# Attention plus token-mixing block: one query shift row folded and summed in one pass, and the output weights split into two parts for twelve matmuls

## The chip, the cores and the metric

The kernel runs on one core of a Trainium2 chip. The metric is the device time of one execution in microseconds (us). Before the change it is 433.37 us, the median of three runs (433.19 to 434.04).

## The reference

The input x has 2048 tokens (rows) of 448 channels. It passes through linear attention and then a mixer that mixes along the tokens; each is preceded by a layer norm whose scale and shift come from a small condition vector c, and each is added back through a gate:

```python
mod = silu(c) @ w_mod             # six rows of 448: sa, ca, ga, sb, cb, gb
h = layernorm(x) * (1 + ca) + sa
x = x + ga * A(h)
h = layernorm(x) * (1 + cb) + sb
x = x + gb * B(h)

def A(h):                         # 16 heads of 28 channels
    q, k, v = split(h @ wqkv)
    pq, pk = phi(q), phi(k)       # phi(t) = (t + 1 if t > 0 else exp(t)) + 1e-6
    kv, z = einsum(pk, v), sum(pk)            # per head, over all tokens
    return (pq @ kv / (pq @ z + 1e-6)) @ wo

def B(h):                         # along the tokens
    return w2.T @ gelu(w1.T @ h + b1) + b2
```

## The kernel before, in words

All arithmetic is in 32 bits. A matmul at full precision ("fp32") takes two passes on the matmul engine (PE). In most places the kernel instead splits each operand into a high part, rounded to the format `fp32r` by a copy on ACT, and a low part, the rest, and adds three products: high by high, high by low, low by high. `split(full, hi, lo)` (L82) makes the parts: a copy on ACT, a subtraction on DVE. A second way leaves DVE out: ACT copies the high part, ACT copies its negative into the low part, and a DMA from POOL's queue adds the full value to it. For the pieces of w1, `split_to` (L319) takes the second way for the pieces in `PIECE_DMA`; `split_end` (L315) issues their DMAs.

Every engine takes its instructions in the order in which the code emits them; there is no planner. Program order is therefore the schedule, and a step that waits holds up all that stands behind it on its engine.

The work has four stages.

1. *Projections and sums over tokens* (L560 to L825). The tokens come in 16 tiles of 128. In the loop `for t in range(4, NT)` (L682) PE projects tile t + 1 to keys (`project(t + 1, 1, "kp")`: ten matmuls, the third of which, "hl", needs the low part of the tile, made on DVE by `a_split_low`, L413), closes tile t (`close`, L437: one matmul with the norm's mean row `Wrow`), and adds an older tile to the four sums of keys by tokens (`a_outer`, L545: eleven matmuls). ACT and DVE turn the projections into phi(k), split them, and normalise and split x. From t = 10 on a query tile is projected per iteration as well (`a_q`).

   The layer norm's shift enters the projections by a row of `Wrow`. For q (j = 0) `row_part` (L275) accumulates on DVE a 128 x 448 tile `accb` of partial sums. In t = 9 `row_sum(0)` (L283: seven fp32r matmuls) and `row_bias(0)` (L289: one fp32 matmul of `sel_b` by `accb`) add everything up in a bank `rowb`, and `row_out(0)` (L292: a copy on ACT, a subtraction on DVE) writes it to `Wrow`.

2. *Joining* (L783 to L985). From the sums come `csum`, then the 112 x 448 products `kvb` (L814), which DVE multiplies by a mask into `kvm`. Wo lies in four parts `wo_sb[g]` of 112 rows, each multiplied on DVE by the gate `mods[2]` (L779, L791). Four fp32 matmuls `wp` (L968) multiply the groups of `kvm` by them. ACT copies each result to `wpg` (L970), eight DMAs from SP's queue regroup the rows into `wpr` (L977), and `wp_split` (L980) splits these into `wph` and `wpl`, which the next stage needs. Between these stand queries (`a_q`), and the pieces of w1, split two at a time (`split_to(2)`, 4, 6, 8).

3. *The loop over tiles* (L987, `for i in range(NT + LAG)`). For tile i, `b_transpose` (L857, writes `tq`) transposes the scaled queries `pn`, `b_high` (ACT) and `b_low`, `b_low_last` (DVE) split the result, and `b_out` (L887, `op`) multiplies it by `wph` and `wpl`. The `pn` of the next tile come from a chain on DVE with one step on POOL: `b_prod`, `b_sum`, `b_eps` (POOL), `b_recip`, `b_scale`. In DVE's order `b_low(i)` stands between `b_sum(i + 1)` and `b_recip(i + 1)`, so it is ahead of `pn` of tile i + 1. Norms, further queries and, from i = 5 on, the first product with w1 (`step`, `up`) are woven in. The iteration ends with `split_to(8 + max(0, i - 5))`.

4. *The mixer* (L1293 to L1333): the products `up` with w1, gelu, and the products `y` with w2.

Tiles of SBUF come from two pools, `slots` (74 buffers) and the smaller `tok` (27 buffers; helper `tslot`); a bank of PSUM comes from a pool of eight.

Of the kernel before, what the change touches and what calls it, by code (L numbers as in the profile page):

```python
# [20 lines left out]
DH = 28  # L21
EPS = 1e-5

PIECE_DMA = range(8, 18)
PRE_LOAD = {14: 2, 15: 4}
KV_LAG = 4
HIGH_AT = {13: (11, 12), 14: (13,), 15: (14, 15)}
# [24 lines left out]
def block_kernel(ctx: ExitStack, tc: tile.TileContext, x, xt, wqkv, wo, w1, b1, w2, c, wmod, wfirst, out):  # L52
# [50 lines left out]
    cst.tile([P, 112], F32, name="space")  # L103
# [12 lines left out]
    sel_s = cst.tile([P, ROWS], F32R, name="sel_s")  # L116
    rowst = []
    for i in range(RING):
        rowst.append(cst.tile([P, P], F32R, name=f"rowst{i}"))
# [115 lines left out]
    def mod_add(j):  # L235
        acc = macc[j]
        nc.vector.tensor_add(acc[:G - 64], acc[:G - 64], acc[64:])

    def mod_high(j):
        acc, both = macc[j], moving(slot, f"mh{j}")  # L240
        macc[j] = (both,)
        nc.scalar.activation(both[:64], acc[:64], AF.Copy)
        return lambda: nc.vector.tensor_sub(both[64:], acc[:64], both[:64].bitcast(F32))
# [43 lines left out]
            nc.tensor.matmul(rowb[j][:ROWS, :D], sel_s, w, start=(i == 0), stop=False)  # L287

    def row_bias(j):  # L289
        nc.tensor.matmul(rowb[j][:ROWS, :D], sel_b, accb.pop(j), start=False, stop=True)  # L290

    def row_out(j):  # L292
        ps, w = rowb.pop(j), Wrow[j]
# [157 lines left out]
    def a_exp(t, ps):  # L451
        a_exp1(t, ps)
        a_relu(t, ps)
# [223 lines left out]
    low()  # L677
    sum_end()
    a_split(7)
    wo_sb = []  # L680
    late = [t for t in range(NT) if t not in Q_EARLY.values()]
    for t in range(4, NT):  # L682
        if 5 < t < NT - 1:
            project(t + 1, 1, "kp")
        kp = close(t, 1) if t > 4 else kps[4]
        if t == 9:
            row_sum(0)
            row_bias(0)
        if t > 4:
            a_outer(t - KV_LAG)  # L690
        if t % 2 and 4 < t < NT - 2:
            a_transpose(t + 1)
        if t in Q_EARLY:
            a_q(Q_EARLY[t])
        if t == 12:
            mp = mod_sum2(2)
        pair = t % 2 and 7 < t + 3 < NT
        if pair:
            first, second, end = a_stats_dve((t + 3, t + 4))
            first(0)  # L700
        if 5 <= t < 9:
            w_low(0, t - 5)
        if pair:
            second(0)
        if 5 <= t < 9:
            row_part(0, t - 5)
        a_phi_q(t in Q_EARLY)
        if t == 9:
            a_exp(t, kp)
        if t % 2 and 4 < t < NT - 2:  # L710
            a_copy(t + 1)
            a_copy(t + 2)
        if t != 9:
            a_exp(t, kp)
        if 7 < t + 3 < NT:
            a_split_high(t + 3)
        a_pk_parts(t - 1)
        highs = HIGH_AT.get(t, (t - 2,))
        for i in highs[:1]:
            a_norm(i)  # L720
            a_high(i)
        if t % 2 == 0 and 4 < t < NT - 3:
            low = a_rows(t + 2)
        if t == 11:
            low2 = mod_high(2)
        for j, i in MOD_AT.get(t, ()):
            mod_add(j) if i is None else mod_part(j, i)
        if t == 14:
            low4()
        a_pk(t, kp)  # L730
        if t % 2 == 0 and 4 < t < NT - 3:
            low()
        if 7 < t + 3 < NT:
# [12 lines left out]
        if 4 <= t < 8:  # L746
            w_high(0, t - 4)
            if t == 7:
                w_row(0)
        if t == 9:  # L750
            row_out(0)
# [8 lines left out]
        if t == 10:  # L760
            mod_add(2)
        if t == 11:
            low2()
        if t == 13:
            low4 = mod_high(4)
        if t in (7, 10):
            load_mod(4 if t == 7 else 3)
        if t == 10:
            load_qkv(2, tslot)
        if t == 8:  # L770
            for g in range(4):
                w = tslot(f"wo{g}", parts=G)
                nc.sync.dma_start(w, wo[g * G:(g + 1) * G, :])
                wo_sb.append(w)
            b12 = cst.tile([P, NF + NT], F32, name="b12")
            nc.sync.dma_start(b12, b1)
            b1c, b2c = b12[:, :NF], b12[:, NF:]
        if t >= 13:
            nc.vector.tensor_mul(wo_sb[t - 13], wo_sb[t - 13], mods[2][:G])  # L779
        load_to(PRE_LOAD.get(t, 0))  # L780


    a_pk_parts(NT - 1)  # L783
    nc.vector.tensor_add(pksum[1], pksum[1], pksum[0])
    zs = (moving(slot, "zh"), moving(slot, "zl"))
    split(pksum[1], *zs)
    load_to(10)
    a_phi_q()
    a_outer(NT - 4)
    a_outer(NT - 3)  # L790
    nc.vector.tensor_mul(wo_sb[3], wo_sb[3], mods[2][:G])  # L791
# [12 lines left out]
    a_q(late.pop(0))  # L804
    csum = []
    for ch in range(4):
        csum.append(slot(f"cs{ch}"))
        nc.scalar.activation(csum[ch], cacc[ch][:, :D], AF.Identity, scale=col[1][:, ch:ch + 1])
        nc.vector.scalar_tensor_tensor(csum[ch], zb, col[0][:, ch:ch + 1], csum[ch], op0=ALU.mult, op1=ALU.add)
    a_phi_q()  # L810
    a_q(late.pop(0))
    split_to(6)
    mp = mod_sum2(4)
    kvb = bank("kvb")  # L814
    for ch in range(4):
# [6 lines left out]
    nc.vector.tensor_mul(kvm, kvb[:G, :D], mask)  # L822
# [7 lines left out]
    pns, phs, ys, opb, sums, nms, nm2s, rss, vss = {}, {}, {}, {}, {}, {}, {}, {}, {}  # L830

    dens, prods, lasts = {}, {}, {}

    def b_prod(t):
# [7 lines left out]
    def b_eps(t):  # L842
        nc.gpsimd.tensor_scalar_add(dens[t], dens[t], 1e-6)  # L843
# [4 lines left out]
    def b_scale(t):  # L848
        pn = pns.pop(t, None) or tslot(f"pn{t}", w=512)
        nc.vector.scalar_tensor_tensor(pn[:, :D].rearrange("p (h d) -> p h d", d=DH),  # L850
                                       pq[t].rearrange("p (h d) -> p h d", d=DH), 1e-6,
                                       dens.pop(t).unsqueeze(2).to_broadcast([P, H, DH]),
                                       op0=ALU.add, op1=ALU.mult)
        pns[t] = pn
        pq[t] = None

    def b_transpose(t):  # L857
        pn = pns.pop(t)
# [101 lines left out]
            del parts[k]  # L960

    a_q(late.pop(0))
    for fn in (b_prod, b_sum, b_eps, b_recip, b_scale):
        fn(0)
    mod_add(3)
    for g in range(4):
        wp = bank(f"wp{g}")
        nc.tensor.matmul(wp[:G, :D], kvm[:, g * G:(g + 1) * G], wo_sb[g], start=True, stop=True)  # L968
        wpg = tslot(f"wpg{g}", parts=G)
        nc.scalar.activation(wpg, wp[:G, :D], AF.Copy)  # L970
        if g == 0:
            Wpr += [tslot(f"wpr{ch}") for ch in range(4)]
        for ch in range(4):
            r0, r1 = max(ch * P, g * G), min(ch * P + P, (g + 1) * G)
            for p0 in (0, 64) if ch == 3 else (0,):
                if r0 < r1:
                    nc.sync.dma_start(Wpr[ch][p0 + r0 - ch * P:p0 + r1 - ch * P], wpg[r0 - g * G:r1 - g * G])  # L977
# [10 lines left out]
    for i in range(NT + LAG):  # L988
# [398 lines left out]
```

## Time and profile before

| | |
|---|---|
| median of three runs | 433.37 us |
| the profiled execution, its own time | 434.09 us |
| its span, from the first to the last instruction | 432.4 us |
| PE busy between 0 and 20 us | 18.89 us |
| PE busy between 20 and 40 us | 19.68 us |
| PE busy between 40 and 310 us | 270.0 of 270.0 us |
| PE busy between 310 and 432 us | 119.34 us |
| DVE busy between 40 and 60 us | 18.82 us |
| ACT busy between 120 and 130 us | 7.25 us |

A row of a timeline holds start and length in us, engine, line of code, instruction, result and operands, shapes, count, and in brackets the idle time of the engine before it with what ended that time. PEld is the load of a matmul's stationary operand. The start of a matmul in a stream is followed by the next 0.20 us later although its row says 0.36 us, since they are pipelined: the pitch from start to start is what one costs. The same holds, less strongly, for ACT and DVE.

### The profile page before, as it was taken

The page shows a single profiled execution, that of the slowest core. Times are in us where ns is not written, and L with a number is a line of the kernel's source. Part 1 is how long each engine was busy: PE and PEld are TensorE (multiplying, and loading weights), DVE is VectorE, ACT ScalarE, POOL GpSimd, SP SyncE. Part 2 cuts the span into 40 slices and gives each one's busy share as a digit, 9 for nine tenths or more (in the row PEclk, how much of TensorE's full clock was granted, in tenths as well). Part 3 has the DMA queues.
Part 4 walks back from the last instruction along what each step waited for, and adds up shares of the span by engine and source line. Part 5 has one row for each costly group of instructions (what it writes and reads, how often), then busy time and mean ns, then how long its engine had stood idle before and what let it go on. Part 6 is the DMA issues. An engine that isn't in the chain of part 4 may idle for free.

```text
span 432.4 us, 7216 instructions
## 1 busy us (share of the span) xinstructions
PE 427.9 (99%) x2331; PEld 398.0 (92%) x2331; DVE 365.1 (84%) x814; ACT 278.9 (65%) x595; POOL 120.1 (28%) x199
## 2 busy tenths in 40 slices
PE   8999999999999999999999999999999999999997
PEld 8888899999899999999999999999999999999996
DVE  4899987889899999998579695739799998898894
ACT  5799869658578899996755263537464664655550
POOL 4345444300026577775200000010113131132010
PEclk9999999999999999999999999999999999999999
DMA  8997997565300036354427461577379977986431
GB/s 282 385 337 162 239 264 162 89 206 193 86 1 0 26 74 148 74 125 97 145 85 244 142 212 50 166 203 210 79 193 214 207 159 159 214 170 144 85 46 41
DMA packets 63797, 66.14 MB, mean 153 GB/s; under 512 B 4816, under 2 KB 55312, under 8 KB 63760
## 3 DMA queue, kind: packets, MB, share of 16 engines
q1 hardware_dynamic: 54688, 50.90, 37.8%
q0 software_dynamic: 8784, 14.32, 20.8%
q10 hardware_dynamic: 288, 0.46, 0.4%
q8 instruction: 18, 0.29, 0.3%
q14 instruction: 19, 0.16, 0.1%
HBM read 46.30 MB, written 7.34 MB: 124 GB/s over the span
## 4 chain that ended last, share of the span: by engine, by line
PE 97%; DVE 1%; ACT 1%; issue 0%
PE y L1183 19%; PE up L951 10%; PE up L950 10%; PE up L952 10%; PE y L1184 9%; PE cacc L554 7%; PE qp L432 7%; PE op L893 7%; PE kp L432 6%; PE op L900 1%; PE warm L188 1%; PE tq L863 1%; PE qp L439 1%; PE kvb L818 1%; PE wp L968 1%; PE rowb L287 1%
## 5 line engine op out<-in xcount | busy, mean ns | idle before, releaser
L950 PE MATMUL up<-h2h,ph 128*128 128x448 f32 x224 | 81.2, 362 | 0.0
L951 PE MATMUL up<-h2l,ph 128*128 128x448 f32 x224 | 81.2, 362 | 0.0
L952 PE MATMUL up<-h2h,pl 128*128 128x448 f32 x224 | 80.8, 361 | 0.0
L1138 POOL DMA_DIRECT2D a<-a x16 | 14.2, 964 | 142.6 <-DMA pr<-in_B_w_dram 76.7
L950 PEld LDWEIGHTS up<-h2h,ph 128*128 128x128 f32 x224 | 42.0, 188 | 3.1
L952 PEld LDWEIGHTS up<-h2h,pl 128*128 128x128 f32 x224 | 41.9, 187 | 3.0
L951 PEld LDWEIGHTS up<-h2l,ph 128*128 128x128 f32 x224 | 42.0, 188 | 2.3
L84 DVE TENSOR_TENSOR pl<-pr,ph 128x512 fp32r<-128x512 f32 x46 | 30.7, 688 | 2.6 <-ACT ph L83 1.7
L1189 ACT ACTIVATE cc<-y 128x448 f32<-128x448 f32 x24 | 13.0, 546 | 26.7 <-PE y L1184 26.7
L1102 DVE TENSOR_TENSOR u<-u,mod 128x448 f32<-128x448 f32 x14 | 8.7, 623 | 23.0 <-ACT u L1101 22.8
L83 ACT ACTIVATE ph<-pr 128x512 fp32r<-128x512 f32 x46 | 27.6, 623 | 0.8 <-PE up L952 0.5
L1101 ACT ACTIVATE u<-up,b 128x448 f32<-128x448 f32 x14 | 8.8, 625 | 25.4 <-PE up L952 24.9
L432 PE MATMUL kp<-wh,hh 128*128 128x448 f32 x64 | 23.8, 377 | 0.0
L554 PE MATMUL cacc<-pkh,xh 128*128 128x448 f32 x64 | 23.6, 369 | 0.0
L432 PE MATMUL qp<-wh,hh 128*128 128x448 f32 x64 | 23.5, 368 | 0.0
L1203 POOL DMA_DIRECT2D out_dram<-yt x14 | 12.7, 909 | 37.3 <-DVE yt L1194 27.9
L843 POOL TENSOR_SCALAR den<-den 128x16 f32<-128x16 f32 x16 | 8.8, 548 | 44.2 <-DVE den L840 44.2
L554 PE MATMUL cacc<-pkl,xh 128*128 128x448 f32 x56 | 20.3, 362 | 0.0
L893 PE MATMUL op<-wph,pth 128*128 128x448 f32 x48 | 18.7, 390 | 0.0
L1144 DVE TENSOR_TENSOR a<-a,s 128x512 f32<-128x512 f32 (+1 forms) x32 | 18.5, 622 | 0.0
L83 ACT ACTIVATE s2h<-s 128x512 fp32r<-128x512 f32 (+1 forms) x16 | 8.3, 569 | 15.5 <-DVE s L1144 15.5
L1183 PE MATMUL y<-ub,a11h 128*128 128x448 f32 x56 | 18.2, 375 | 0.0
(235 smaller groups left out, 1383.7 us busy)
## 6 DMA issues: line engine op xcount, KB each, us to landing
pr<-in_B_w_dram SPq DMA_DIRECT2D x56, 256.0 KB, 3.1
a<-in_B_w_dram SPq DMA_DIRECT2D x32, 256.0 KB, 4.8
a<-in_B_w_dram SPq DMA_DIRECT2D x32, 192.0 KB, 4.7
xt<-in_xt_dram SPq DMA_DIRECT2D x16, 256.0 KB, 5.0
x<-in_A_x_dram SPq DMA_DIRECT2D x16, 224.0 KB, 5.0
wm<-in_B_wmod_dram SPq DMA_DIRECT2D x16, 196.0 KB, 5.2
out_dram<-x SPq DMA_DIRECT2D x14, 224.0 KB, 2.3
out_dram<-yt POOLq DMA_DIRECT2D x14, 224.0 KB, 6.1
```

The costliest lines, as they stand in the source:

```text
L83: nc.scalar.activation(hi, full, AF.Copy)
L84: nc.vector.tensor_sub(lo, full, hi.bitcast(F32))
L432: nc.tensor.matmul(pps[t, j][:, :D], a[:, ch * P:(ch + 1) * P], w, start=first, stop=False)
L554: nc.tensor.matmul(cacc[ch][:, :D], a[:, s], b, start=(t == 0 and i == 0), stop=(t == NT - 1 and i == len(todo) - 1))
L893: nc.tensor.matmul(opb[t][:, :D], a, b, start=(ch == n == 0), stop=False)
L950: nc.tensor.matmul(ps[:, :D], hi[:, sl], mh, start=first, stop=False)
L951: nc.tensor.matmul(ps[:, :D], hi[:, sl], ml, start=False, stop=False)
L952: nc.tensor.matmul(ps[:, :D], lo[:, sl], mh, start=False, stop=last)
L1138: nc.gpsimd.dma_start(w, a, accum_op=ALU.add)
L1144: nc.vector.tensor_tensor(w, raw2[q, a][i], raw2[q, b][i], op=op)
L1183: nc.tensor.matmul(ps[:, :D], h[:, s], w, start=opens and r == 0, stop=False, skip_group_check=True)
L1184: nc.tensor.matmul(ps[:, :HD], l[:, s], wh, start=False, stop=closes and r == PAIRS - 1, skip_group_check=True)
```

## The change

- *The query's shift row.* At the end of t = 8 `row_fold(0)` adds, on DVE, the lower 64 rows of `accb` to the upper 64. In t = 9 `row_high(0)` copies the 64 rows as a high part (ACT), copies `sel_b` to an fp32r tile `sel_r` (ACT), and subtracts the low part into the other 64 rows (DVE). `row_bias(0)` is then one fp32r matmul. `row_sum(0)` and `row_bias(0)` move from t = 9 to t = 10, behind `project(11)` and ahead of `close(10)`; `row_out(0)` follows that. In t = 9 `a_exp` moves ahead.
- *The sum of the gate row.* `mod_add(2)` moves from the end of t = 10 into t = 11.
- *Wo.* The products with `mods[2]` on DVE go. `wo_split` makes a high and a low part of each `wo_sb[g]`: two copies on ACT, one adding DMA from POOL's queue, in t = 14, t = 15 and, for two, behind the loop. The parts lie in the smaller pool.
- *kvm* is split too (ACT, DVE), and twelve fp32r matmuls replace four fp32 ones. The factor `mods[2]` comes in afterwards: DVE multiplies each result into `wpg` where ACT copied it.
- *Order.* The chain of `pn` of tile 0 moves from behind the `wp` stage to ahead of it. Of the pieces of w1, 4 is split just ahead of the `wp` matmuls, 5 between two `wp_split`, and 6 and 7 at the end of iteration i = 0, by the second way (`PIECE_DMA` now begins at 6).

```diff
-PIECE_DMA = range(8, 18)
+PIECE_DMA = range(6, 18)
...
     def row_bias(j):
-        nc.tensor.matmul(rowb[j][:ROWS, :D], sel_b, accb.pop(j), start=False, stop=True)
+        nc.tensor.matmul(rowb[j][:ROWS, :D], sel_r if j == 0 else sel_b, accb.pop(j), start=False, stop=True)
+
+    def row_fold(j):
+        acc = accb[j]
+        nc.vector.tensor_add(acc[:64], acc[:64], acc[64:])
+
+    def row_high(j):
+        acc, both = accb[j], moving(tslot, f"rb{j}")
+        nc.scalar.activation(both[:64], acc[:64], AF.Copy)
+        nc.scalar.activation(sel_r, sel_b, AF.Copy)
+        accb[j] = both
+        return lambda: nc.vector.tensor_sub(both[64:], acc[:64], both[:64].bitcast(F32))
...
+    def wo_split(g):
+        full, hi, lo = wo_sb[g], moving(tslot, f"woh{g}", parts=G), moving(tslot, f"wol{g}", parts=G)
+        nc.scalar.activation(hi, full, AF.Copy)
+        nc.scalar.activation(lo, hi.bitcast(F32), AF.Copy, scale=-1.0)
+        nc.gpsimd.dma_start(lo, full, accum_op=ALU.add)
+        wo_sb[g] = None
+        wos.append((hi, lo))
...
         if 5 < t < NT - 1:
             project(t + 1, 1, "kp")
-        kp = close(t, 1) if t > 4 else kps[4]
-        if t == 9:
+        if t == 10:
             row_sum(0)
             row_bias(0)
+        kp = close(t, 1) if t > 4 else kps[4]
+        if t == 10:
+            row_out(0)
...
+        if t == 9:
+            a_exp(t, kp)
+            row_high(0)()
...
+        if t > 13:
+            wo_split(t - 14)
...
         if t == 11:
+            mod_add(2)
             low2 = mod_high(2)
...
             low()
+        if t == 8:
+            row_fold(0)
         if 7 < t + 3 < NT:
             a_split_low(t + 3)
...
-        if t >= 13:
-            nc.vector.tensor_mul(wo_sb[t - 13], wo_sb[t - 13], mods[2][:G])
...
     a_pk_parts(NT - 1)
+    for g in (2, 3):
+        wo_split(g)
...
-    split_to(6)
+    b_prod(0)
+    b_sum(0)
+    b_eps(0)
     mp = mod_sum2(4)
...
     a_phi_q()
+    b_recip(0)
+    mod_out(4, mp)
     kvm = slot("kvm", parts=G)
     nc.vector.tensor_mul(kvm, kvb[:G, :D], mask)
-    mod_out(4, mp)
+    b_scale(0)
+    kvh, kvl = slot("kvh", dt=F32R, parts=G), slot("kvl", dt=F32R, parts=G)
+    split(kvm, kvh, kvl)
     load_to(PRE + MID + 3)
-    split_to(8)
...
     a_q(late.pop(0))
-    for fn in (b_prod, b_sum, b_eps, b_recip, b_scale):
-        fn(0)
     mod_add(3)
+    split_to(5)
+    wps = [bank(f"wp{g}") for g in range(4)]
+    for gs in ((0, 1), (2,), (3,)):
+        for i, (a, b) in enumerate(((kvh, 0), (kvh, 1), (kvl, 0))):
+            for g in gs:
+                nc.tensor.matmul(wps[g][:G, :D], a[:, g * G:(g + 1) * G], wos[g][b], start=(i == 0), stop=(i == 2))
     for g in range(4):
-        wp = bank(f"wp{g}")
-        nc.tensor.matmul(wp[:G, :D], kvm[:, g * G:(g + 1) * G], wo_sb[g], start=True, stop=True)
         wpg = tslot(f"wpg{g}", parts=G)
-        nc.scalar.activation(wpg, wp[:G, :D], AF.Copy)
+        nc.vector.tensor_mul(wpg, wps[g][:G, :D], mods[2][:G])
...
             for ch in range(4):
                 wp_split(ch)
+                if ch == 1:
+                    split_to(6)
```

More of the change, by code (lines that the diff above doesn't have):

```diff
@@ L101, in make_mask @@
                                 pattern=[[0, 4], [DH, 4], [0, DH]], channel_multiplier=-1)
-    cst.tile([P, 112], F32, name="space")
+    cst.tile([P, 14], F32, name="space")
     mhalf = cst.tile([P, 2], F32, name="mhalf")
@@ L116, in block_kernel @@
     sel_s = cst.tile([P, ROWS], F32R, name="sel_s")
+    sel_r = cst.tile([P, ROWS], F32R, name="sel_r")
     rowst = []
@@ L679, in block_kernel @@
     a_split(7)
-    wo_sb = []
+    wo_sb, wos = [], []
+    def wo_split(g):
[5 more added lines that the diff above has]
+        wos.append((hi, lo))
     late = [t for t in range(NT) if t not in Q_EARLY.values()]
@@ L707, in block_kernel @@
         a_phi_q(t in Q_EARLY)
-        if t == 9:
-            a_exp(t, kp)
         if t % 2 and 4 < t < NT - 2:
@@ L749, in block_kernel @@
                 w_row(0)
-        if t == 9:
-            row_out(0)
         if t == 12:
@@ L759, in block_kernel @@
             mod_part(2, t - 7)
-        if t == 10:
-            mod_add(2)
         if t == 11:
@@ L777, in block_kernel, with b_prod, b_sum, b_eps @@
             b1c, b2c = b12[:, :NF], b12[:, NF:]
-        if t >= 13:
-            nc.vector.tensor_mul(wo_sb[t - 13], wo_sb[t - 13], mods[2][:G])
         load_to(PRE_LOAD.get(t, 0))
+    pns = {}
+    dens, prods, lasts = {}, {}, {}
+    def b_prod(t):
+        prods[t] = tslot(f"pd{t}")
+        nc.vector.scalar_tensor_tensor(prods[t], pq[t], 1e-6, zb, op0=ALU.add, op1=ALU.mult)
+    def b_sum(t):
+        dens[t] = small.tile([P, H], F32, name=f"den{t}", tag="den")
+        nc.vector.tensor_reduce(dens[t], prods.pop(t).rearrange("p (h d) -> p h d", d=DH), axis=AX.X, op=ALU.add)
+    def b_eps(t):
+        nc.gpsimd.tensor_scalar_add(dens[t], dens[t], 1e-6)
+    def b_recip(t):
+        nc.vector.reciprocal(dens[t], dens[t])
+    def b_scale(t):
+        pn = pns.pop(t, None) or tslot(f"pn{t}", w=512)
+        nc.vector.scalar_tensor_tensor(pn[:, :D].rearrange("p (h d) -> p h d", d=DH),
+                                       pq[t].rearrange("p (h d) -> p h d", d=DH), 1e-6,
+                                       dens.pop(t).unsqueeze(2).to_broadcast([P, H, DH]),
+                                       op0=ALU.add, op1=ALU.mult)
+        pns[t] = pn
+        pq[t] = None
     a_pk_parts(NT - 1)
+    for g in (2, 3):
+        wo_split(g)
     nc.vector.tensor_add(pksum[1], pksum[1], pksum[0])
@@ L790, in block_kernel @@
     a_outer(NT - 3)
-    nc.vector.tensor_mul(wo_sb[3], wo_sb[3], mods[2][:G])
     for i in (2, 3):
@@ L820, in block_kernel @@
     a_phi_q()
+    b_recip(0)
+    mod_out(4, mp)
     kvm = slot("kvm", parts=G)
     nc.vector.tensor_mul(kvm, kvb[:G, :D], mask)
-    mod_out(4, mp)
+    b_scale(0)
+    kvh, kvl = slot("kvh", dt=F32R, parts=G), slot("kvl", dt=F32R, parts=G)
+    split(kvm, kvh, kvl)
     load_to(PRE + MID + 3)
-    split_to(8)
     Wpr, Wph, Wpl = [], [], []
     H2h, H2l = [None] * NT, [None] * NT
-    pns, phs, ys, opb, sums, nms, nm2s, rss, vss = {}, {}, {}, {}, {}, {}, {}, {}, {}
-    dens, prods, lasts = {}, {}, {}
-    def b_prod(t):
-        prods[t] = tslot(f"pd{t}")
-        nc.vector.scalar_tensor_tensor(prods[t], pq[t], 1e-6, zb, op0=ALU.add, op1=ALU.mult)
-    def b_sum(t):
-        dens[t] = small.tile([P, H], F32, name=f"den{t}", tag="den")
-        nc.vector.tensor_reduce(dens[t], prods.pop(t).rearrange("p (h d) -> p h d", d=DH), axis=AX.X, op=ALU.add)
-    def b_eps(t):
-        nc.gpsimd.tensor_scalar_add(dens[t], dens[t], 1e-6)
-    def b_recip(t):
-        nc.vector.reciprocal(dens[t], dens[t])
[L848 to L855, printed above, removed]
+    phs, ys, opb, sums, nms, nm2s, rss, vss = {}, {}, {}, {}, {}, {}, {}, {}
     def b_transpose(t):
```

## The prediction

> **What bounds the kernel now.** I read the page first, then the chain that ended last, then busy time by stretches, and last the timelines around the two places that the change touches. The page, and the chain's share by engine and line:
>
> ```profile
> span 432.4 us, 7216 instructions
> PE 427.9 (99%) x2331; PEld 398.0 (92%) x2331; DVE 365.1 (84%) x814; ACT 278.9 (65%) x595; POOL 120.1 (28%) x199
> PE 97%; DVE 1%; ACT 1%; issue 0%
> 130.00:145.00 15.00, 15.00 (x80) 13.96 (x79) 14.73 (x36) 12.33 (x29) 8.89 (x16) 1.00 0.00 1
> ```
>
> PE is the bound: it is idle for 4.5 us in all. So a microsecond of matmul that goes comes off the end, if PE isn't made to wait elsewhere. The fourth row (busy time from 130 to 145 us: PE, PEld, DVE, ACT, POOL) says where that is in doubt: in the loop over tiles DVE works 14.73 of 15.00 us. There PE can't get ahead of DVE; it can only use up the margin between them.
>
> **What PE saves.** The chain in order of time:
>
> ```profile
> 49.06 1.42 PE rowb L287 x7
> 50.48 0.75 PE rowb L290 x2
> 108.81 3.01 PE wp L968 x8
> ```
>
> Seven fp32r matmuls take 1.42 us, 0.20 each. The fp32 one of the shift row takes 0.75 us in two passes, and the four of `wp` 3.01. One fp32r matmul for the first saves 0.75 - 0.20 = 0.55 us; twelve for the four save 3.01 - 2.40 = 0.60. Together PE is rid of 1.15 us. The Trainium skill ("FP8 and Floating Point Precision", TensorE Precision Notes) says that true fp32 makes four passes; at 4 x 0.20 the saving would be 1.40. The trace shows two longer ones, and decides.
>
> **Iterations 8 to 10: most of the 0.55 us is lost.** Before, the shift row's sum stood ahead of `project(11)`; now it stands behind it, so PE comes to that projection 1.42 + 0.75 = 2.17 us sooner. Its third matmul needs the low part of tile 11 ("hl"), and `row_fold` is put just ahead of that on DVE, which is working without a gap:
>
> ```profile
> 53.80 0.36 PE L432 MATMUL kp<-wh,hl 128*128 128x448 f32 x1
> 50.64 0.16 DVE L398 TENSOR_TENSOR rowst<-mv,rowst 128x4 fp32r<-128x4 f32 x1
> 50.71 0.69 DVE L415 TENSOR_TENSOR hl<-xt,hh 128x512 fp32r<-128x512 f32 x1
> 61.72 0.62 DVE L237 TENSOR_TENSOR acc<-acc 48x448 f32<-48x448 f32 x1
> 62.26 0.62 DVE L380 BATCH_NORM_STATS2 st<-x 128x6 f32<-128x448 f32 x1
> ```
>
> The matmul's place moves from 53.80 to 51.63. An addition of this kind holds DVE for 62.26 - 61.72 = 0.54 us, so hl starts at 51.25 and ends at 51.94. How soon PE follows is shown by tile 8, where it waited:
>
> ```profile
> 41.84 0.68 DVE L415 TENSOR_TENSOR hl<-xt,hh 128x512 fp32r<-128x512 f32 x1
> 42.58 0.19 PEld L432 LDWEIGHTS kp<-wh,hl 128*128 128x128 f32 x1 [0.19 <-DVE hl L415]
> 42.89 0.36 PE L432 MATMUL kp<-wh,hh 128*128 128x448 f32 x1
> ```
>
> hl ended at 42.52; the matmul behind it began at 42.89, so the hl matmul's own place was 42.69, 0.17 us after. For tile 11 that is 51.94 + 0.17 = 52.11: a stall of 0.48 us. PE leaves t = 10 only 0.07 us ahead. The rest here is covered: the two copies on ACT fall into its idle 1.8 us ahead of the row below, and DVE makes up for its subtraction in its own pauses before 57 us.
>
> ```profile
> 53.59 0.57 ACT L407 ACTIVATE hl<-rw 34x128 fp32r<-34x128 f32 x2 [1.82 <-PE rw L404]
> 91.66 0.58 ACT L500 ACTIVATE xh<-xn 128x448 fp32r<-128x448 f32 x1 [1.71 <-DVE xn L496]
> 96.28 0.58 ACT L83 ACTIVATE zh<-pk 128x448 fp32r<-128x448 f32 x1 [2.62 <-PE cacc L554]
> 109.78 0.29 POOL L843 TENSOR_SCALAR den<-den 128x16 f32<-128x16 f32 x1 [26.39 <-DVE den L840]
> ```
>
> **Wo's parts** cost nothing: two copies of about 0.58 us (as L83's row) fit into a pause of ACT like the 1.71 us at 91.66, of which each of t = 14 and 15 has one, four fit into the 2.62, and POOL, whose queue takes the four DMAs, is idle for 26 us. Without that cover each copy would delay `xh` and then `a_outer`. DVE is rid of four multiplications there; it isn't the one waited for at that point. `mod_add(2)` has one answer too: its reader stands late in t = 11.
>
> **From the wp matmuls to wph: 0.26 us later.** They start at 108.65 (row below) - 0.07 = 108.58. The parts of `kvm` are there: `kvm` begins at 106.68, and the two splits after it end by 108.5, before the fifth matmul, the first to need the low part. That one starts at 109.38, and its result can be read about 0.40 later, at 109.78. DVE meanwhile has `kvm`, `b_scale`, the low part (from 107.9, when ACT has the high one), `mod_add(3)` and piece 4 to do; at the pitch of 0.54 above that lasts until about 109.55 (an estimate): 0.2 us of cover. Then the multiplication, 0.63 as in L822's row, against 0.55 for ACT's copy:
>
> ```profile
> 108.65 3.17 PE L968 MATMUL wp<-wo,kvm 112*112 112x448 f32 x8
> 106.68 0.63 DVE L822 TENSOR_TENSOR kvm<-kvb,mask 112x448 f32<-112x448 f32 x1 [0.24 <-issue]
> 109.60 0.55 ACT L970 ACTIVATE wpg<-wp 112x448 f32<-112x448 f32 x1 [2.45 <-PE wp L968]
> 110.17 5.12 SPq L977 DMA_DIRECT2D wpr<-wpg  x8
> 117.05 0.58 ACT L83 ACTIVATE wph<-wpr 128x448 fp32r<-128x448 f32 x1 [0.66 <-DMA wpr<-wpg]
> 119.25 0.49 ACT L871 ACTIVATE pth<-tq 128x384 fp32r<-128x384 f32 x1 [1.63 <-PE tq L863]
> ```
>
> The first `wpg` is done at 110.41 instead of 110.15. From there SP issues eight DMAs of 0.64 us without a gap, and the last `wph` waits for the last of them; three later `wpg` are in time for their issues. So the last `wph` moves from 117.05 to 117.31. That PE is 0.6 us quicker through the stage doesn't help: SP's issues set its end.
>
> **Behind it four copies stand where ACT had 1.63 us of idle time: 0.86 us later.** The iteration's last step now copies pieces 6 and 7, two copies each, and `b_high(1)` (L871) is behind them in ACT's queue. Their pace:
>
> ```profile
> 149.54 0.62 ACT L326 ACTIVATE ph<-pr 128x512 fp32r<-128x512 f32 x1
> 150.19 0.63 ACT L327 ACTIVATE pl<-ph 128x512 fp32r<-128x512 f32 x1
> 150.90 0.49 ACT L871 ACTIVATE pth<-tq 128x384 fp32r<-128x384 f32 x1
> 96.76 1.13 ACT L83 ACTIVATE ph<-pr 128x512 fp32r<-128x512 f32 x2
> ```
>
> A low part follows its high part by 0.65 us, since it reads it; two independent copies are 1.13 - 0.62 = 0.51 apart. The block takes 0.65 + 0.51 + 0.65 + 0.51 = 2.32 us. It can't take less than 4 x 0.51 = 2.04; the upper bound is rival 3. It starts 0.48 after `wph` (as 96.76 does after 96.28), at 117.79, so `b_high(1)` starts at 120.11 instead of 119.25: 0.86 later.
>
> **DVE passes that on to PE.** `b_low(1)`, which waits for `b_high(1)`, is ahead of the `pn` in DVE's queue, and from there DVE runs without a pause that matters. Each `tq` needs its `pn`:
>
> ```profile
> 120.21 0.56 DVE L878 TENSOR_TENSOR ptl<-tq,pth 128x384 fp32r<-128x384 f32 x1 [0.20 <-ACT pth L874]
> 127.01 0.63 DVE L850 SCALAR_TENSOR_TENSOR pn<-pq,den 128x448 f32<-128x448 f32 x1
> 132.28 0.62 DVE L850 SCALAR_TENSOR_TENSOR pn<-pq,den 128x448 f32<-128x448 f32 x1
> 128.42 0.60 PE L863 MATMUL tq<-ident,pn 128*128 128x128 f32 x4
> 133.29 0.49 PE L863 MATMUL tq<-ident,pn 128*128 128x128 f32 x3
> 145.52 0.62 DVE L909 SCALAR_TENSOR_TENSOR x<-op,x 128x448 f32<-128x448 f32 x1 [0.44 <-PE op L900]
> ```
>
> The `pn` of tiles 3 and 4 end at 127.64 and 132.90; with 0.86 of delay and the 0.17 that PE takes to follow, their `tq` can start at 128.67 and 133.93. Before they started at 128.42 and 133.29: +0.25 and +0.64. PE, which would come 0.67 us early (0.07 + 0.60), waits at the first transposes for 0.67 + 0.64 = 1.31 us in all. At 145.52 DVE itself waits for PE, so the lateness stops growing there; and since PE has no idle time until its last 3 us, nothing gives it back.
>
> **Sum.** -1.15 (PE) + 0.48 (hl) + 1.31 (`tq`) = +0.64 us. The profiled execution, 434.09 us for a span of 432.4, would become 434.7; it lies 0.7 above the median of 433.37, from which the forecast is 434.0. About 0.2% (0.87 us) is what a measurement of this kernel can tell from no change; the forecast lies within it.
>
> **Rivals.**
> (1) *The whole saving arrives:* 433.37 - 1.15 = 432.2. For it, PE's 97% of the chain. Against it, the `pn` done at 132.90 leaves PE 0.39 us at 133.29, so `wph` and ACT's block would have to come about 0.9 us sooner than before, while SP's eight issues alone begin later.
> (2) *No stall at tile 11* (if DVE gains 0.5 us before 50.7): then the wp stage is 0.48 sooner, the delay of 0.86 becomes 0.38, and the end +0.16, 433.5. Against it, DVE's rows are gapless there.
> (3) *Slower: the four copies take longer.* ACT's next copy after a low part starts 0.71 after it (150.90 after 150.19). It may be waiting for PE there, but no row shows that pace without such a wait. At 0.65 + 0.71, twice, the block takes 2.72 us, and the end is +1.04, 434.4. It decides from 2.55 on, where the end passes 0.87.
> (4) *POOL slows DVE.* In i = 1 POOL issues the DMAs of pieces 6 and 7 while DVE makes `pn`. Beside a mask step of POOL a normalisation took 0.88 us instead of 0.51:
>
> ```profile
> 75.90 0.72 POOL L98 TENSOR_SCALAR_AFFINE_SELECT mask<-mask 112x448 f32<-112x448 f32 x1
> 76.00 0.88 DVE L496 TENSOR_SCALAR xn<-x,mv 128x448 f32<-128x448 f32 x1
> 80.70 0.51 DVE L496 TENSOR_SCALAR xn<-x,mv 128x448 f32<-128x448 f32 x1
> 81.61 0.90 POOL L528 DMA_DIRECT2D pkl<-pk  x1 [4.21 <-ACT pkl L527]
> 81.84 0.55 DVE L506 TENSOR_TENSOR xl<-xn,xh 128x384 fp32r<-128x384 f32 x1
> ```
>
> Two operations at 0.37 more give +1.4, 434.8. Against it, beside a DMA issue (81.61) `xl` took 0.55 for 384 columns, in step with the 0.62 of 61.72 for 448. The Trainium skill ("SBUF — State Buffer", Who interferes with whom) has the rule: DVE and GpSimd share a port pair, and one blocks the other. By it a DVE operation with two SBUF inputs is held only by a GpSimd instruction that reads SBUF; the mask row agrees, and no row shows that issuing a DMA does this.
>
> **How the numbers follow.** The forecast has 0.45, the rivals in their order 0.15, 0.13, 0.22 and 0.05. Faster takes rival 1: 0.15. Slower takes rivals 3 and 4 and that part of the forecast (0.05) that an error of 0.25 us in it puts above 0.87: 0.32. The rest, 0.53, is no change that can be told. The forecast's own range is 433.5 to 434.4. To hold the time 8 times in 10 the range goes from 432.5, where half of what I count as lost is kept, to 434.9, just beyond rival 4; it leaves out rival 1.
>
> **What would show it.** In the changed profile: L290 one matmul at 0.20 pitch and the twelve at 0.20; a PEld wait for hl of about 0.5 us near 51.6; PE waits for `pn` at the first `tq` past 120 us; the last `wph` near 117.3 and then L326/L327 twice ahead of L871, itself near 120.1; the end about 0.6 us later. The forecast is wrong if PE's idle time stays near 4.5 us, if `tq` never waits, or if L871 comes before 119.2.

## The result and the profile after

The changed kernel takes 437.56 us, the median of seven runs (436.21 to 439.88), against 434.22 for the kernel before on the same chip (seven runs, 433.19 to 434.36): a ratio of 1.0082, 95% interval 1.0064 to 1.0100. That is 3.6 us slower (0.0082 x 434), and 434.9 was the end of the forecast's range. The profiled execution is the longest of the seven, 439.88 us with a span of 438.2; it shows more loss than the median has.

The forecast's own steps are there. First the rows around tile 11, from the timeline of the changed kernel:

```profile
50.11 0.62 DVE L295 TENSOR_TENSOR accb<-accb 64x448 f32<-64x448 f32 x1
50.82 0.69 DVE L427 TENSOR_TENSOR hl<-xt,hh 128x512 fp32r<-128x512 f32 x1
50.85 0.37 PE L444 MATMUL kp<-wl,hh 128*128 128x448 f32 x1
51.57 0.47 PE L444 MATMUL kp<-wh,hl 128*128 128x448 f32 x1 [0.35 <-DVE hl L427]
51.87 0.36 PE L444 MATMUL kp<-wh,hh 128*128 128x448 f32 x1
```

The row of hl starts at 51.57 and the next at 51.87, so hl's own place was 51.67; behind 50.85 it would have been 51.05. That is a stall of 0.62 us, where 0.48 was forecast. Then ACT's block ahead of `b_high(1)`, and the first `tq` that wait:

```profile
121.07 0.58 ACT L83 ACTIVATE wph<-wpr 128x448 fp32r<-128x448 f32 x1 [0.66 <-DMA wpr<-wpg]
121.56 0.61 ACT L338 ACTIVATE ph<-pr 128x512 fp32r<-128x512 f32 x1
122.20 0.64 ACT L339 ACTIVATE pl<-ph 128x512 fp32r<-128x512 f32 x1
122.74 0.61 ACT L338 ACTIVATE ph<-pr 128x512 fp32r<-128x512 f32 x1
123.39 0.64 ACT L339 ACTIVATE pl<-ph 128x512 fp32r<-128x512 f32 x1
123.93 0.47 ACT L901 ACTIVATE pth<-tq 128x384 fp32r<-128x384 f32 x1
131.68 0.63 DVE L825 SCALAR_TENSOR_TENSOR pn<-pq,den 128x448 f32<-128x448 f32 x1
132.46 0.63 PE L893 MATMUL tq<-ident,pn 128*128 128x128 f32 x4 [0.24 <-DVE pn L825]
```

The four copies take 123.93 - 121.56 = 2.37 us (forecast 2.32), and PE waits for `pn`. So far the reading holds. But what the second fence shows stands almost 4 us later than forecast: the last `wph` is at 121.07 instead of 117.31. Two things that the forecast doesn't have come ahead of it. The first is in t = 11; the timelines of DVE and PE, and busy time by stretches (PE, PEld, DVE, ACT, POOL, then the granted clock, the share of the DMA engines and GB/s):

```profile
63.21 0.62 DVE L238 TENSOR_TENSOR acc<-acc 48x448 f32<-48x448 f32 x1
69.99 0.45 DVE L231 TENSOR_SCALAR acc<-wm,sc 112x448 f32<-112x448 f32 x1 [6.16 <-DMA pk<-pk]
75.24 0.44 PE L254 MATMUL modp<-mh,ones_r 128*128 128x448 f32 x1 [1.93 <-DVE mh L244]
78.11 0.57 PE L444 MATMUL kp<-wh,hl 128*128 128x448 f32 x1
78.48 0.57 PE L444 MATMUL kp<-wh,hh 128*128 128x448 f32 x1
70.00:80.00 10.00, 8.07 (x33) 7.03 (x32) 9.46 (x21) 5.14 (x10) 5.32 (x7) 0.83 0.42 70
```

DVE waits 6.16 us before the first operation on `acc4`, the accumulator of the fifth gate row. In the kernel before it waited 0.40, and for PE:

```profile
64.44 0.45 DVE L230 TENSOR_SCALAR acc<-wm,sc 112x448 f32<-112x448 f32 x1 [0.40 <-PE cacc L554]
```

`acc4` takes a freed buffer of the pool `slots`. In the compiled kernel before that is the one of `pkh` of tile 7, which PE has nearly read. With the row part `accb0` is read later (by `row_high` in t = 9, no longer by the matmul at the top of it), and `acc4` gets the buffer of `pk` of tile 9, which an adding DMA of POOL's queue must still read. PE stands 1.93 us, and then its clock is lowered for some three microseconds (0.83 in the mean of these 10 us): the matmuls at 78.11 and 78.48 are 0.37 apart, not 0.20.

The second is small and everywhere. The chain in order of time, first before, then after, shows ten matmuls of a projection:

```profile
101.02 2.00 PE qp L432 x10
116.57 2.00 PE qp L432 x10
```
```profile
134.93 2.05 PE qp L444 x10
140.44 2.05 PE qp L444 x10
```

Ten of the same instructions take 2.05 us for 2.00. The same already holds where nothing of the change has been reached (timelines of PE, after and then before; 0.82 us over four matmuls, 0.60 over three):

```profile
20.02 0.37 PE L444 MATMUL kp<-wh,hh 128*128 128x448 f32 x1
...
20.84 0.36 PE L444 MATMUL kp<-wh,hh 128*128 128x448 f32 x1
```
```profile
22.48 0.36 PE L432 MATMUL kp<-wh,hh 128*128 128x448 f32 x1
...
23.08 0.37 PE L432 MATMUL kp<-wl,hh 128*128 128x448 f32 x1
```

### The profile page after: what moved, and what is told of

Its sections match the earlier page's. It is cut to its first block, busy times and chain, and to the rows that moved or that the text cites. A ratio compares the mean times of both kernels' runs of the same rounds, so it can differ in the third digit from the quotient of the medians.

```text
span 438.2 us, 7244 instructions
## 1 busy us (share of the span) xinstructions
PE 431.0 (98%) x2334; PEld 396.6 (91%) x2334; DVE 365.7 (83%) x815; ACT 284.8 (65%) x604; POOL 126.6 (29%) x205
## 4 chain that ended last, share of the span: by engine, by line
PE 69%; DVE 3%; ACT 1%; issue 1%; DMA 1%; SPq 0%; ACTq 0%
PE y L1217 19%; PE up L980 10%; PE up L982 10%; PE up L981 10%; PE y L1218 9%; PE op L923 6%; PE qp L444 1%; PE op L930 1%; PE tq L893 1%; DMA wpr<-wpg 1%; DVE pq L482 0%; DVE wpg L1002 0%; PE y L1214 0%; DVE ptl L908 0%; DVE pn L825 0%
## 5 line engine op out<-in xcount | busy, mean ns | idle before, releaser
L84 DVE TENSOR_TENSOR pl<-pr,ph 128x512 fp32r<-128x512 f32 x44 | 29.6, 687 | 3.1 <-ACT ph L83 2.1
L83 ACT ACTIVATE ph<-pr 128x512 fp32r<-128x512 f32 x44 | 26.4, 618 | 0.8 <-PE up L982 0.5
L444 PE MATMUL kp<-wh,hh 128*128 128x448 f32 x64 | 24.7, 391 | 0.1
L1217 PE MATMUL y<-ub,a12h 128*128 128x448 f32 x56 | 18.2, 374 | 0.0
```

Source lines behind the costliest of these rows:

```text
L83: nc.scalar.activation(hi, full, AF.Copy)
L84: nc.vector.tensor_sub(lo, full, hi.bitcast(F32))
L444: nc.tensor.matmul(pps[t, j][:, :D], a[:, ch * P:(ch + 1) * P], w, start=first, stop=False)
L1217: nc.tensor.matmul(ps[:, :D], h[:, s], w, start=opens and r == 0, stop=False, skip_group_check=True)
```

## The experiments

**First four: is it the reused buffer?** The theory (T) was that the wait of `acc4` is the loss. In the kernel `e1_acc4_small_pool` it has a buffer of the smaller pool:

```diff
-            macc[j] = (tslot if j == 5 else slot)(f"acc{j}", parts=G)
+            macc[j] = (tslot if j in (4, 5) else slot)(f"acc{j}", parts=G)
```

> The changed kernel with one word more: the accumulator acc4 of mod_part(4, 0) comes from the smaller pool, so that it does not take over a buffer that an adding DMA still reads. Theory T (the loss is that buffer): the 6.16 us wait of VectorE's first acc4 operation in tile 11 and TensorE's 1.93 us wait at the first matmul of mod_sum2(2) are gone, and the time is what is left of the forecast, the hl stall of about 0.6 and the ACT block, near 434.9 us, a ratio of 1.000 to 1.003 to the kernel before. Rival U (the Wo part or a slower pace of TensorE makes the loss, the wait is a feature of one profile): it stays at 436.5 to 437.5 us, ratio 1.006 to 1.009.

`e2_row_part_alone` is the kernel before with `row_fold`, `row_high`, `sel_r`, the sum in t = 10 and `mod_add(2)` in t = 11, and with `sel_r` the shorter tile `space` (below); nothing else of the change is in it:

```diff
+        if t == 10:
+            row_sum(0)
+            row_bias(0)
...
+            row_high(0)()
...
+            mod_add(2)
...
+            row_fold(0)
```

> The kernel before with the shift-row part alone (row_fold, row_high, sel_r, the sum in tile 10, mod_add(2) moved to tile 11); the Wo part is as before. Theory T: accb0's buffer is released one tile later, the acc4 operation in tile 11 waits for a landing DMA, and the time is 436 to 437.5 us, ratio 1.004 to 1.008, with TensorE waiting over 1 us at mod_sum2(2). Rival U: no such loss, hl stall and the cheaper row matmul about cancel, 434.0 to 434.5 us, ratio 0.999 to 1.001.

`e3_wo_part_alone` is the changed kernel with those lines undone, except for `mod_add(2)` and the tiles `sel_r` and `space`:

```diff
-        if t == 10:
+        if t == 9:
             row_sum(0)
             row_bias(0)
...
-            row_high(0)()
...
-            row_fold(0)
```

> The changed kernel with its row part undone (the fp32 row matmul, the sum in tile 9, a_exp(9) back in its place); the Wo part and the move of mod_add(2) stay. Theory T: no wait of the acc4 operation, no hl stall; what is left is the ACT block of about 1 us less the 0.60 us of the twelve matmuls, 434.2 to 435.2 us, ratio 1.000 to 1.002. Rival U: the loss stays, 436.5 to 437.5 us, ratio over 1.005.

`e4_buffer_fold_pieces` has e1's edit, `row_fold` behind `a_split_low(11)`, and pieces 6 and 7 out of ACT's block:

```diff
-        if t == 8:
-            row_fold(0)
         if 7 < t + 3 < NT:
             a_split_low(t + 3)
+        if t == 8:
+            row_fold(0)
...
+            split_to(7)
             mod_out(3, mod_sum2(3))
...
-        split_to(8 + max(0, i - 5))
+        split_to((6, 6, 7)[i] if i < 3 else 8 + max(0, i - 5))
```

> The changed kernel with three mends: acc4 from the smaller pool, row_fold behind a_split_low(11), and the four copies of pieces 6 and 7 taken out of the block ahead of b_high(1) (piece 6 at i = 2, the later ones from i = 3 on). Theory T: no acc4 wait, no hl stall, L871 starts about 1 us earlier against the last wph copy, and the saving of 1.15 us shows for the greater part: 433.0 to 433.9 us, ratio 0.997 to 0.9995, faster than both. Rival U: still over 436 us.

| kernel | median us | ratio | 95% interval |
|---|---|---|---|
| e1_acc4_small_pool | 436.94 | 1.0073 | 1.0060 to 1.0085 |
| e2_row_part_alone | 437.24 | 1.0088 | 1.0074 to 1.0101 |
| e3_wo_part_alone | 437.45 | 1.0090 | 1.0076 to 1.0103 |
| e4_buffer_fold_pieces | 434.91 | 1.0038 | 1.0024 to 1.0051 |

T falls. In e1 the wait of DVE is gone, and 0.7% is still lost; e3 has neither that wait nor the row part and is as slow; e4 has no wait of PE after its first 30 us, and is slower than before. (e2's time lies in T's range, 436 to 437.5, but PE waited 0.40 us there, not over 1, so that is luck.) Rival U was right that the loss stays. It named the Wo part or a slower pace of PE: the first falls, since e2 has none of it and loses as much. Something that all four share must cost 2 us and more, and each shows projections of 2.05.

What they share is one edit that the prediction's reading passed over, and that the diff ahead of it leaves out, in the tiles of the constants:

```diff
-    cst.tile([P, 112], F32, name="space")
+    cst.tile([P, 14], F32, name="space")
...
+    sel_r = cst.tile([P, ROWS], F32R, name="sel_r")
```

`space` is read by nobody; it only pushes what lies behind it. 14 words and `ROWS` = 98 make 112 again, but in the compiled program each of these tiles starts at a multiple of 32 bytes: 56 bytes take 64, 392 take 416, together 480 where 112 words took 448. What lies behind `sel_r`, the last constants and then the smaller pool, is 32 bytes further on. The weights of the projections and of `op`, the moving operands there, are in that pool, taken from word 16 of a buffer by `moving` (L76).

**Second four: is it the shift?** (theory P) `g1_before_shifted` is the kernel before with the length of `space`, the spacer, changed, so that nothing but the place differs:

```diff
-    cst.tile([P, 112], F32, name="space")
+    cst.tile([P, 120], F32, name="space")
```

> The kernel before with its unused spacer 8 words longer (120 for 112) and nothing else: the same instructions, with the smaller pool and what is allocated behind it 32 bytes further on, where the changed kernel has them. Theory P (the pace: matmuls whose moving operand lies in the smaller pool take 0.2052 us instead of 0.2005, because that operand then starts 32 bytes off a multiple of 64): the project and output matmuls go to 0.205 and the time to 436.0 to 437.0 us, ratio 1.006 to 1.008, without any change of the work. Rival (the slower pace comes from the new instructions, or from the chip): pace and time as before, ratio 0.999 to 1.001.

`g2_after_moving_aligned`, on the changed kernel:

```diff
-        return new(name, dt=dt, parts=parts, w=512)[:, 16:16 + D]
+        a = 24 if new is tslot else 16
+        return new(name, dt=dt, parts=parts, w=512)[:, a:a + D]
```

> The changed kernel with the 448 moving columns taken from word 24 instead of word 16 of every buffer of the smaller pool: pool and buffers stay where they are, the moving operands alone start at a multiple of 64 bytes again. Theory P, if the moving operand's start is what counts: pace back to 0.2005, time 434.0 to 435.0 us, ratio 1.001 to 1.004. Rival within P (another tile of the shifted pools counts, such as rowst, wpr or the scalars of the constants): it stays near 437, ratio over 1.006.

`g3_after_aligned`, on the changed kernel, and `g4_mended_aligned`, the same edit on e4:

```diff
-    cst.tile([P, 14], F32, name="space")
+    cst.tile([P, 6], F32, name="space")
```

> The changed kernel with the spacer at 6 words for 14, so that the smaller pool starts where it does in the kernel before. Theory P: all of the 2.9 us of slower pace comes back, and what is left is the forecast: hl stall, ACT block and perhaps the wait of acc4, 434.0 to 435.0 us, ratio 1.001 to 1.004. Rival: stays near 437, ratio over 1.006.

> The kernel with the three mends (acc4 from the smaller pool, row_fold behind a_split_low(11), pieces 6 and 7 out of the block), ratio 1.0038, with the spacer at 6 words. Theory P: no waits of TensorE are left and the pace is 0.2005, so that the 1.15 us of saved TensorE time show, 431.6 to 432.6 us, ratio 0.996 to 0.998, faster than both. Rival: as without the alignment, about 434.9.

| kernel | median us | ratio | 95% interval |
|---|---|---|---|
| g1_before_shifted | 435.98 | 1.0059 | 1.0046 to 1.0072 |
| g2_after_moving_aligned | 436.78 | 1.0074 | 1.0059 to 1.0090 |
| g3_after_aligned | 435.27 | 1.0040 | 1.0026 to 1.0053 |
| g4_mended_aligned | 432.68 | 0.9982 | 0.9973 to 0.9991 |

g1 settles that the shift costs: the instructions of the kernel before, 32 bytes further on, take 2.5 us more (P's range began at 436.0, and 435.98 was measured). Its chain shows where; the matmuls of `cacc`, whose moving operand is in `slots`, keep their pace, 55 in 11.01, as before the change (second fence: the kernel before):

```profile
84.48 2.04 PE qp L432 x10
86.94 11.01 PE cacc L554 x55
98.34 2.05 PE qp L432 x10
```
```profile
85.00 2.00 PE qp L432 x10
87.41 11.01 PE cacc L554 x55
98.82 2.00 PE qp L432 x10
```

In g3 the projections are back at 2.00, and g4 beats both kernels; both end just above their ranges, by 0.3 and 0.1 us. g2 ends 1.8 us above its range: its profiled run, the slowest of six, has the wait of `acc4` again (6.02 us), and its projections take 2.04, not 2.00, so that a multiple of 64 bytes is not enough.

The same run shows that the clock need not fall after such a wait. PE stands 1.90 us at the same matmul as in the changed kernel, and goes on at 0.20:

```profile
75.12 0.44 PE L255 MATMUL modp<-mh,ones_r 128*128 128x448 f32 x1 [1.90 <-DVE mh L245]
76.21 0.37 PE L445 MATMUL kp<-wl,hh 128*128 128x448 f32 x1
76.42 0.36 PE L445 MATMUL kp<-wh,hl 128*128 128x448 f32 x1
76.62 0.37 PE L445 MATMUL kp<-wh,hh 128*128 128x448 f32 x1
```

**Third four: what is left, and whose place counts?** `g5_aligned_acc4_small` is g3 with e1's edit:

> The changed kernel with the spacer at 6 words and acc4 from the smaller pool: neither the shift nor the reused buffer; hl stall and ACT block stay. Theory B+P (shift and buffer are all that the forecast missed): 434.0 to 434.5 us, ratio 1.001 to 1.0025, what the forecast's own sum of +0.64 says, and runs no further apart than those of before. Rival (something else is missed): 435 us and more, ratio over 1.0035.

`g7_row_alone_aligned` is e2 with the spacer at 6:

> The row part alone on the kernel before, with the spacer at 6 words. By the forecast's sums -0.55 for the matmul and +0.6 for the hl stall, so 433.4 us, plus the wait of acc4 on the landing DMA, which costs TensorE nothing when it is about 3.5 us long and 0.7 us when 4.5: 433.6 to 434.6 us, ratio 1.0005 to 1.0025, and over 2 us less than the same kernel with the pool shifted (1.0088). Rival (shift makes no difference here): near 437.

`h1_after_word40` is e1 with `a = 40` in g2's edit:

> The changed kernel, pool still shifted by 32 bytes, with the moving columns from word 40 of every buffer of the smaller pool and acc4 from that pool: the moving operand starts 64 bytes past a multiple of 128, as in the kernel before; from word 24 it started at a multiple of 128. Theory M (the place of the moving operand's start modulo 128 bytes sets the pace): 0.2005 us for project and output matmuls, 434.2 to 435.0 us, ratio 1.002 to 1.0035. Rival O (the moving operand's place explains only a part, the rest comes from other tiles of the shifted pools, which other engines read and write): pace 0.202 to 0.204, ratio 1.004 to 1.007.

`h2_before_word24` is the kernel before with g2's edit:

> The kernel before with the moving columns from word 24 of every buffer of the smaller pool, and nothing else: no pool moves, the moving operands alone start 32 bytes off a multiple of 64. Theory M: pace 0.205 in the project and output matmuls, 435.5 to 436.5 us, ratio 1.005 to 1.007. Rival O: less than half of that, ratio under 1.003.

| kernel | median us | ratio | 95% interval |
|---|---|---|---|
| g5_aligned_acc4_small | 434.26 | 1.0021 | 1.0011 to 1.0030 |
| g7_row_alone_aligned | 435.56 | 1.0047 | 1.0029 to 1.0065 |
| h1_after_word40 | 435.51 | 1.0044 | 1.0032 to 1.0056 |
| h2_before_word24 | 435.95 | 1.0047 | 1.0035 to 1.0059 |

h2 moves no tile; moving operands alone bring most of the loss. g5 is the forecast's own case, and comes out at 0.9 us slower (0.5 to 1.3), where the forecast had 0.64. g7 came out 1 us above its range; its profiled run, the slowest of six, waits 5.88 us for the DMA, not 3.5, and PE 1.95, but how long the other five waited isn't on record. h1 lies in O's range, with projections of 2.02; whether other tiles cause this, as O says, the next runs decide.

**Last five: which place?** `i1_constants_shifted` has the spacer at 120 words and 24 unused words ahead of `b12`; `i2_pools_shifted_64` the spacer at 128; both on the kernel before. `g6_wo_alone_aligned` is e3 with the spacer at 6.

```diff
+            cst.tile([P, 24], F32, name="space2")
             b12 = cst.tile([P, NF + NT], F32, name="b12")
```

> The kernel before with the spacer 8 words longer and an unused tile of 24 words further on: the constants between the two lie 32 bytes further on, the smaller pool and all behind it 128 bytes, so that its moving operands start at the same place modulo 128. Theory M (the moving operands of the smaller pool): pace and time as before, ratio 0.999 to 1.001. Rival O (the small constants, which every engine reads, take a part): pace 0.2015 to 0.203 in the project matmuls, ratio 1.002 to 1.004.

> The kernel before with the spacer 16 words longer: everything behind it 64 bytes further on, so that moving operands of the smaller pool start at a multiple of 128 instead of 64 past one. If the place modulo 64 counts: as before, ratio 0.999 to 1.001. If the place modulo 128 counts: a slower pace, 0.202 to 0.204, ratio 1.003 to 1.006, and the rest of the slow pace with word 24 (1.0074) is explained by it.

> The Wo part and the move of mod_add(2) alone, spacer at 6 words, row part undone. By the forecast's sums 0.86 + 0.64 or so of late output matmuls less 0.60 for the twelve matmuls, and no hl stall and no acc4 wait: 433.9 to 434.6 us, ratio 1.0005 to 1.002, 2.5 us less than the same kernel with the pool shifted (1.009). Rival (the Wo part hides a further loss): 435.2 and more, ratio over 1.0035.

i1: 434.68 us, ratio 1.0024 (1.0014 to 1.0033). i2: 435.19, 1.0038 (1.0026 to 1.0051). g6: 435.62, 1.0043 (1.0029 to 1.0057), with runs from 433.61 to 437.22.

i1 looks as if the constants counted, but it moves the smaller pool too, by 128 bytes. So two more on the kernel before: `i4_before_word48`, g2's edit with `a = 48`, moves the moving operands alone by those 128 bytes; `i5_constants_only`, i1 with `space2` at 120 words, shifts the constants by 32 bytes and the pool by 512.

> The kernel before with the moving columns from word 48 of every buffer of the smaller pool: no pool and no constant moves, the moving operands alone start 128 bytes further on, at the same place as in the run with the constants shifted. Theory M2 (the pace goes by the start of the moving operand modulo 256 or 512 bytes, the constants have no part): pace 0.2015 to 0.2025 in the project matmuls, ratio 1.0015 to 1.0035. Theory C (the constants shifted by 32 bytes made that run slower): as before, ratio 0.999 to 1.001.

> The kernel before with the constants shifted by 32 bytes and the smaller pool by 512 in all, so that its buffers stand at the same place modulo 512 as before. Theory M2: pace and time as before, ratio 0.999 to 1.001. Theory C: pace 0.2015 to 0.2025, ratio 1.0015 to 1.0035.

i4: 434.52 us, ratio 1.0016 (1.0008 to 1.0025). i5: 433.39, 0.9995 (0.9986 to 1.0004). Shifting the constants by 32 bytes costs nothing, and h1's pace needs no other tile: in i4 the moving operands alone bring it. Sorted by the byte at which the moving operands of the smaller pool start, modulo 256 (i5 differs from the kernel before by 512, so no run tells 256 from 512), and leaving out up to three longer groups of each run:

| start modulo 256 | kernels | ten matmuls of a projection, us | ratio of kernels like the one before but for the place |
|---|---|---|---|
| 192 | before, g3, g5, i5 | 2.00 to 2.02 | 0.9995 (i5) |
| 64 | h1, i1, i4 | 2.02 to 2.04 | 1.0016 (i4), 1.0024 (i1) |
| 0 | g2, i2 | 2.03 to 2.05 | 1.0038 (i2) |
| 224 | after, e4, g1, h2 | 2.04 to 2.07 | 1.0047 (h2), 1.0059 (g1) |

A row of the chain for each of i5, i4, i2 and h2, in this order:

```profile
97.79 2.00 PE qp L432 x10
```
```profile
98.33 2.02 PE qp L433 x10
```
```profile
98.69 2.03 PE qp L432 x10
```
```profile
98.49 2.05 PE qp L433 x10
```

g6 missed too, and lies in its rival's range. Its projections take 2.00, but in its profiled run the last `wph` waited for a late DMA, and ACT, with the four copies behind it, passed that on. In g5 the same wait was 0.65 us:

```profile
118.35 0.58 ACT L83 ACTIVATE wph<-wpr 128x448 fp32r<-128x448 f32 x1 [2.38 <-DMA wpr<-wpg]
118.83 0.62 ACT L338 ACTIVATE ph<-pr 128x512 fp32r<-128x512 f32 x1
123.34 0.44 PE L927 MATMUL op<-wph,pth 128*128 128x448 f32 x1 [1.39 <-ACT rq L478]
125.70 0.57 PE L920 MATMUL op<-wpl,pth 128*128 128x448 f32 x1
```
```profile
116.80 0.58 ACT L83 ACTIVATE wph<-wpr 128x448 fp32r<-128x448 f32 x1 [0.65 <-DMA wpr<-wpg]
```

g5 has the whole Wo part too and takes 434.26 us, so the Wo part need not cost this. Why that DMA is late in one run and not in another stays open, and with it the Wo part's own median.

## Why the prediction was wrong

The table follows one and the same matmul through the profiles: its start minus its start in the kernel before, in us. The first column shows what a run gained or lost at its beginning, before any edit but the shift acts; differences between columns are what counts.

| run | 45 us | 60 | 105 | 118 | 140 | 205 | 425 |
|---|---|---|---|---|---|---|---|
| after | -0.63 | -0.44 | +3.68 | +3.30 | +4.53 | +5.32 | +5.83 |
| g1 (shift alone) | -0.95 | -0.80 | -0.38 | -0.19 | +0.25 | +1.03 | +1.54 |
| g5 (neither shift nor buffer) | -0.63 | -0.46 | -0.52 | -1.08 | +0.11 | +0.11 | +0.11 |
| g4 (mended) | -0.78 | -1.32 | -1.29 | -1.85 | -1.46 | -1.49 | -1.48 |

- *The sum of +0.64* is right for what it counts: g5 goes from -0.63 to +0.11, +0.74. Its terms: tile 11 with the cheaper row matmul +0.17 (forecast -0.07, the stall being longer), the `wp` stage -0.56 (forecast -0.60), the first `tq` +1.19 (forecast +1.31). The first and the last are off by +0.24 and -0.12, so it is in part luck that the sum fits so well.
- *The list that the sum is made of* is the step that failed: it follows the work and the order of the change, and the spacer and `sel_r` have no term at all, as if they cost nothing. The shift that they make costs g1 2.5 us: -0.95 to +1.54, spread over the whole time in which weights from the smaller pool move. After 205 us g1 loses another 0.5, which h2 doesn't (1.04 at 205 and at 425), so there it is not these moving operands; the mixer's tiles behind the pool are shifted in g1 and not in h2. The loss comes after 305 us, in the products `y`: 0.45 in those whose moving operand is a tile `ut`, some of which lie behind the pool, and 0.05 in those with a tile `ub`, which all lie there and keep their pace (0.211 us for 128 x 448 in both kernels). So the shift does not slow every matmul whose moving operand it moves, and which tile counts there was not tried.
- *"`mod_add(2)` has one answer too"*, and the fold at the end of t = 8: the order of work was followed, the reuse of buffers was not. That the row part turns it is shown: in e2 `acc4` lies in the buffer of `pk` of tile 9 and waits 4.45 us, in e3, where `mod_add(2)` moves too, it lies where it did and waits 0.44 for PE. That it is the later read of `accb0` that does it is only argued. In the profiled run this is the step from -0.44 to +3.68, 4.1 us, less 0.4 for the shift (g1 in the same stretch); about 1.5 of it is the lowered clock (ten matmuls in 3.58 us, for 2.05). It differs from run to run: DVE's wait was 3.48 us in g3, 4.45 in e2, 6.16 after, and PE's 0, 0.40 and 1.93, so some 3.5 to 4.2 us of it are covered. In the medians it is worth 0.8 us without the shift (1.0040 for g3, 1.0021 for g5) and 0.4 with it (1.0082 after, 1.0073 for e1); in both pairs the intervals overlap.
- *Shares.* The shift 2.3 us (1.0073 for e1, 1.0021 for g5), the buffer 0.8, the forecast's own terms 0.9: 4.0 us, where 3.6 was measured with an interval of 2.8 to 4.3. Other pairs give 1.8 us (after and g3, e2 and g7) to 2.5 (before and g1) for the shift.
- *Rival 1* (the whole saving) lost to the two stalls that the forecast named: with both taken out, g4 gains 0.7 us of the 1.15 (-0.78 to -1.48), and the rest goes at `tq` (+0.39 from 118 to 140). Rival 2 needed no hl stall, and there was one. Rival 3 did not happen, since the block took 2.37 us; rival 4 was not tried by itself, and g5's term for `tq`, 1.19 for 1.31, leaves nothing for it. (Its mask row is no case of an operation with two SBUF inputs: by L496 `xn` reads one tensor, and `mv` as scalars.) The slower end that came was none of the rivals.
- *The range* began at 432.5, said to keep half of what is counted as lost. Half of 0.48 + 1.31 kept gives 433.1, so that end does not follow from its reason; the time missed the other end.

## What to carry to other kernels

A line that computes nothing still places everything behind it: before costing the work of a change, add up what it does to the addresses, with the rounding of each tile, and make the kernel before with only that shift as the first experiment. A changed lifetime is an edit too, since it turns the order in which a tight pool hands out its buffers; ask of each tile near the change whose buffer it takes over, and what must still read that. When every stall is accounted for and the time still doesn't fit, compare the pace of equal instructions in a stretch that the change does not touch.

## What the hardware showed that was not expected

- The pace of the projections' and `op`'s matmuls, 128 x 448 fp32r, depends on the byte at which the moving operand starts: about 0.200, 0.202, 0.203 and 0.205 us at 192, 64, 0 and 224 modulo 256. Other places were not tried, and the mixer's products of `ub` did not follow this. The Trainium skill ("SBUF — State Buffer", Operand start alignment) asks for a multiple of the element size only, and says that this is about legality, not speed; the runs here show the speed.
- The granted clock can fall to half (0.50 between 76 and 78 us) after short pauses of PE. After 1.93 us of idle time ending at 75.24 the matmuls were 0.37 us apart, and after 1.95 in g7 and 1.39 in g6 too; after 1.90 in g2 and 0.40 in e2 they kept 0.20. The Trainium skill ("TensorE: Matmul & The Clock Gate", Part 1) gives a window of about 3.4 us; shorter pauses were enough in three runs here. The length of the pause alone does not decide: a stall of 1.9 us cost itself in g2, and some 1.5 us more in the changed kernel.
- The adding DMA that frees `acc4`'s buffer made DVE wait 3.48 to 6.16 us in different runs, too wide a spread to plan with one profile.
